# A decay built in two column parts, and four score banks for three pairs of heads, in a fused attention and two-layer MoE kernel

## Chip, cores and metric

One core of a Trainium2 chip. The metric is the device time of one execution in microseconds (us), lower is better; before the change it is 803.99 us, the median of three runs (802.63 to 804.92).

## What is computed

Attention over 32 heads (4 batches of 8), 576 tokens, head size 64, with a causal mask and a forget gate `f`; then a feed-forward layer with squared ReLU, then a second one whose hidden row goes through a softmax, a product and a layer norm:

```
scores = q @ k.T / sqrt(D)
cum    = cumsum(log(clip(f, 1e-4, 1)))
scores = where(causal, -1e9, scores + cum[:, None] - cum[None, :])
x      = softmax(scores) @ v            # 2304 x 512
g      = s * max(x @ w_in, 0)**2 + b    # first MoE, hidden size 2048
x2     = g @ w_out
h      = x2 @ w2_in                     # second MoE, hidden size 1024
out    = layer_norm(h * softmax(h)) * g_ln @ w2_out
```

## The kernel before

Heads go in 16 pairs. A pair's 576 query rows are taken in four groups: group 0 holds the query blocks 0 and 1 (256 keys at most), group 1 the last 64 rows of both heads (all 576 keys), groups 2 and 3 the blocks of 384 and 512 keys. For a group, TensorE (PE) multiplies q by k into two PSUM banks `S0` and `S1` (function `scores`, one bank a head), VectorE (DVE) adds the mask, negates and keeps each row's minimum (`unit`, L665, called a minimum below), ScalarE (ACT) takes the exponential (L710), PE transposes the result into a `PT` bank (L725), ACT or DVE copies it to `pa` or `pb` (L732, L733), and PE multiplies by v into the bank `O` (`pv`, L787).

For the first four pairs (`p < NA`, NA = 4) the decay is added on PE: a second, short product of a selector `sel` or `selt` with `dk` gives each score its key's decay. `dk` comes from one chain at the start. `f` of all 32 heads is loaded (32 x 576), clamped on DVE (L421), its logarithm taken on ACT (L423), summed along the keys by a scan on DVE (L432), and from that `decay` makes `dk384` (group 0 and 2, L428 and L429, against key 192) and `dk576` (group 1 and 3, against key 448); each is split in two rows of numbers and then copied to the other half of the partitions (L399 or L401). Later pairs take their decay from `dec` and `dect`, which are loaded from DRAM; `decay_rows` (L444) writes those rows through the `raw` tiles.

Group 0 of all four pairs goes first, then the other groups pair by pair. PSUM has, beside S, PT and O, one bank `h` and two banks of `x2` that belong to the MoE. While only group 0 of the first four pairs runs (`part`), scores go round four banks: `S0`, `S1` and the two of `x2`. All other scores use the two S banks.

The order on each engine's queue is set by a planner (`Plan.run`): every step has an engine or a choice of engines, a cost and a priority, and the planner lists the steps in the order in which its own model would start them. Every engine then runs its list strictly in order, and SyncE (SP) issues all DMAs from one list. Where PE would be idle the planner puts in products with a zero matrix (L488, called fillers). While attention runs, the weights of the MoE are loaded as 64-bit words and converted (`value`: L821 on ACT, L823, L825 and L828 on DVE), and jobs of the first MoE run between the pairs (L1064 into `h`, L1070 to L1072 into `x2`). After attention PE works on the MoEs alone.

Of the kernel before, what the change touches and what calls it, by code (L numbers as in the profile page):

```python
# [12 lines left out]
ALU = mybir.AluOpType  # L13
# [14 lines left out]
BP = 300  # L28
# [33 lines left out]
def f32(ap):  # L62
    return ap.bitcast(F32)
# [184 lines left out]
def dve2(n):  # L248
    return 69 + 0.52 * n
# [14 lines left out]
def kernel(  # L264
# [143 lines left out]
    def tt(out, a, b, n, op, r, w, pri=0):  # L408
# [2 lines left out]

    ft, one, n_ = (es[i][0:BH] for i in (1, 2, 3))
    sel_ = es[0][:, 0:BH]

    dma(ft, f.rearrange("b h s -> (b h) s"), (), [("e", 1)], BH * S * 4, -1e6)
    add("DVE", 60, lambda: nc.vector.memset(eps, 1e-9), (), ["eps"], -9e6)
    add("ACT", 1500, lambda: nc.scalar.activation(out=sm0[:, 0:1], in_=eps, func=AF.Ln), ["eps"], ["sm0"], -9e6)
    add("DVE", 200, lambda: nc.vector.memset(one, 1.0), (), [("e", 2)])  # L420
    add("DVE", 370, lambda: nc.vector.tensor_scalar(out=ft, in0=ft, scalar1=1e-4, scalar2=1.0, op0=ALU.max, op1=ALU.min),  # L421
        (), [("e", 1)], -1e5, lk=True)
    add("ACT", 573, lambda: nc.scalar.activation(out=ft, in_=ft, func=AF.Ln), (), [("e", 1)], -1e5)  # L423

    def decay(g, n0):
        t, w = dks[g], dks[g].shape[1]
        n, at = n_[:, 0:w], n_[:, n0:n0 + 1]
        nc.vector.tensor_scalar(out=t[0:BH], in0=n, scalar1=at, scalar2=None, op0=ALU.subtract)  # L428
        nc.vector.scalar_tensor_tensor(out=t[BH:2 * BH], in0=n, scalar=at, in1=f32(t)[0:BH], op0=ALU.subtract, op1=ALU.subtract)  # L429

    def decays():
        nc.vector.tensor_tensor_scan(out=n_, data0=one, data1=ft, initial=0.0, op0=ALU.mult, op1=ALU.subtract)  # L432
        decay(0, 192)

    add("DVE", 1250 + dve2(384) + dve(384), decays, [("e", 1), ("e", 2)], [("e", 3), ("dk", 0, 0)], -1e5, lk=True)
    add("DVE", dve2(S) + dve(S), lambda: decay(1, 448), [("e", 3)], [("dk", 1, 0)], 3000, lk=True)
    for g, b in enumerate((-1e5, 3000)):
        t = dks[g]
        copy(lambda t=t: t[2 * BH:4 * BH], lambda t=t: f32(t)[0:2 * BH], t.shape[1], [("dk", g, 0)], [("dk", g, 2)], b)
# [10 lines left out]
    decay_rows(0, 256, S, ((dec_d, 0, 0, 512),), "decA")  # L450
    decay_rows(1, 448, S, ((dect_d, 0, 0, S),), "decB")
# [67 lines left out]
    def split_qk(p, part, b):  # L519
# [4 lines left out]
        tt(lambda: t, lambda: r, lambda: f32(h()), n, ALU.subtract, kr + kh, kt, b)  # L524

    add("ACT", 1400, lambda: nc.scalar.activation(out=ms[0][0:BH, 0:1], in_=ft[:, 0:1], func=AF.Exp),
        [("e", 1), ("dk", 0, 2)], [("m", 0)], -9e4)

    def take(keys):

# [24 lines left out]
    def prep_dec(p):  # L555
        j = p % 2
        t, u = decs[j], dects[j]
        kd = [("decA", 0)]
        dma(t[:, :, 0:512], dec_d[p][None].broadcast_to((128, 2, 512)), kd, [("dec", j)], 524288, BP, rate=300, after=[sc_[p - 2, 1]])
        for x in range(2):  # L560
            dma(u[64 * x:64 * x + 64], dect_d[p, x][None].broadcast_to((64, S)), [("decB", 0)], [("dect", j, x)], 256 * S, BP, rate=300, after=[sc_[p - 2, 1]])
# [14 lines left out]
        add("POOL", pool2(64), lambda: nc.gpsimd.tensor_tensor(out=u[:, 512:S], in0=u[:, 512:S], in1=maskt[:, 224:288], op=ALU.add),  # L576
            ["maskt"], [("dect", j, x) for x in range(2)], BP)
# [8 lines left out]
    def scores(p, g):  # L586


        j, qbs = p % NA, [units[i][0] for i in groups[g]]
        part = g == 0 and p < NA  # L590
        one_ = p < NA
        t, h = ((lambda: whole[j]),) * 2 if one_ else ((lambda: ts[j]), (lambda: hs[j]))
        rk = [(a, j, x) for a in (("W",) if one_ else ("T", "H")) for x in ((0,) if g == 0 else PARTS)]
        if one_:
            rk += [("dk", g % 2, y) for y in (0, 2)] + [("selt", p % 2) if g == 1 else "sel"]
        (sx, kx), (sy, ky) = bank("S", part), bank("S", part)

# [24 lines left out]
        def s_mm():
            n = 2 if one_ else 3
            for i in range(n):
# [28 lines left out]
    def unit(s, p, i, two):  # L653
# [864 lines left out]
```

## Time and profile before

| | before |
|---|---|
| median of three runs | 803.99 us |
| the profiled execution | 801.1 us |
| its span, first to last instruction | 799.3 us |
| PE, DVE, ACT busy in the span | 98%, 59%, 62% |

The profiled execution took 801.1 us, of which 1.8 us lie outside the span; it is 2.9 us (0.36%) below the median of the runs shown. Times in the rows count from the span's start. The granted TensorE clock reads 0.999 over the span. A busy PE is a PE with a product under way, and that is not a PE at its peak.

### The profile page before, as it was taken

The page shows a single profiled execution, that of the slowest core. Times are in us where ns is not written, and L with a number is a line of the kernel's source. Part 1 is how long each engine was busy: PE and PEld are TensorE (multiplying, and loading weights), DVE is VectorE, ACT ScalarE, POOL GpSimd, SP SyncE. Part 2 cuts the span into 40 slices and gives each one's busy share as a digit, 9 for nine tenths or more (in the row PEclk, how much of TensorE's full clock was granted, in tenths as well). Part 3 has the DMA queues.
Part 4 walks back from the last instruction along what each step waited for, and adds up shares of the span by engine and source line. Part 5 has one row for each costly group of instructions (what it writes and reads, how often), then busy time and mean ns, then how long its engine had stood idle before and what let it go on. Part 6 is the DMA issues. An engine that isn't in the chain of part 4 may idle for free.

```text
span 799.3 us, 12785 instructions
## 1 busy us (share of the span) xinstructions
PE 779.5 (98%) x4543; PEld 642.2 (80%) x4543; DVE 474.9 (59%) x1025; ACT 495.8 (62%) x1012; POOL 126.6 (16%) x171
## 2 busy tenths in 40 slices
PE   8899999999999999999999999999999999999997
PEld 7567788778788987888878888788998788888886
DVE  8888889778783463321358765522229975665630
ACT  7788798878786676664477677645425654443441
POOL 1323222222110020100102200100002730100000
PEclk9999999999999999999999999999999999999999
DMA  8976897986943784130276875751416121000011
GB/s 273 297 230 221 264 321 243 289 300 227 286 173 121 215 284 136 36 129 1 80 236 232 273 259 185 262 238 57 128 56 235 54 66 39 22 19 27 26 40 53
DMA packets 73015, 132.59 MB, mean 166 GB/s; under 512 B 7704, under 2 KB 29848, under 8 KB 72952
## 3 DMA queue, kind: packets, MB, share of 16 engines
q1 hardware_dynamic: 72952, 131.78, 49.6%
q8 instruction: 35, 0.57, 0.3%
q14 instruction: 28, 0.23, 0.1%
HBM read 91.17 MB, written 40.58 MB: 165 GB/s over the span
## 4 chain that ended last, share of the span: by engine, by line
PE 83%; DVE 5%; issue 4%; ACT 4%; DMA 3%; POOL 1%; ACTq 0%; POOLq 0%; DVEq 0%; SPq 0%
PE h L1064 15%; PE x L1064 9%; PE ph L1273 7%; PE x2w L1072 7%; PE x2w L1070 6%; PE x2w L1071 6%; PE S L628 4%; PE po L1331 4%; PE po L1329 4%; PE po L1330 4%; PE PT L725 4%; PE O L787 4%; PE pt L1317 2%; PE x L1070 2%; PE x L1071 2%
## 5 line engine op out<-in xcount | busy, mean ns | idle before, releaser
L1012 DVE SCALAR_TENSOR_TENSOR gl<-r,b_sb,gh 128x512 fp32r<-128x512 f32 x71 | 55.2, 778 | 133.3 <-ACT gh L1021 128.1
L710 ACT ACTIVATE e<-e,m 128x128 f32<-128x128 f32 (+4 forms) x144 | 83.2, 580 | 20.8 <-DVE m L665 20.6
L1071 PE MATMUL x2w<-gl,u 128*128 128x512 f32 (+1 forms) x200 | 73.7, 368 | 0.0
L1072 PE MATMUL x2w<-gh,u 128*128 128x512 f32 (+1 forms) x200 | 73.7, 368 | 0.0
L1070 PE MATMUL x2w<-gh,u 128*128 128x512 f32 (+1 forms) x200 | 73.6, 368 | 0.0
L725 PE MATMUL PT<-ident,e 128*128 128x128 f32 x384 | 60.0, 281 | 4.1 <-ACT e L710 3.2
L1064 PE MATMUL h<-xhl,w 128*128 128x256 f32 (+1 forms) x384 | 61.0, 297 | 0.5 <-ACT r L998 0.5
L998 ACT ACTIVATE r<-h 128x512 f32<-128x512 f32 x46 | 27.3, 593 | 53.6 <-PE h L1064 53.3
L1329 PE MATMUL po<-v,dh 128*128 128x512 f32 x144 | 58.3, 405 | 0.0
L1331 PE MATMUL po<-v,dl 128*128 128x512 f32 x144 | 56.4, 392 | 0.0
L1330 PE MATMUL po<-v,dh 128*128 128x512 f32 x144 | 56.2, 390 | 0.0
L725 PEld LDWEIGHTS PT<-ident,e 128*128 128x128 f32 x384 | 42.0, 141 | 16.8 <-ACT e L710 7.4
L1321 DVE TENSOR_TENSOR dl<-pt,dh 128x512 fp32r<-128x512 f32 x36 | 24.6, 689 | 49.9 <-ACT dh L1320 49.9
L1064 PEld LDWEIGHTS h<-xhl,w 128*128 128x128 f32 x384 | 49.8, 190 | 2.9 <-ACT r L998 0.7
L1005 ACT ACTIVATE r<-r,s_sb 128x512 f32<-128x512 f32 x68 | 49.3, 724 | 2.2
L1064 PE MATMUL h<-xh,u 128*128 128x256 f32 (+1 forms) x216 | 46.1, 331 | 0.0
L1021 ACT ACTIVATE gh<-r,b_sb 128x512 fp32r<-128x512 f32 x62 | 44.7, 721 | 1.7 <-DVE r L1002 0.4
L1004 ACT ACTIVATE r<-r 128x512 f32<-128x512 f32 x68 | 43.0, 632 | 1.5
L1071 PEld LDWEIGHTS x2w<-gl,u 128*128 128x128 f32 x200 | 37.7, 189 | 6.3
L1072 PEld LDWEIGHTS x2w<-gh,u 128*128 128x128 f32 x200 | 37.7, 189 | 6.2
L1070 PEld LDWEIGHTS x2w<-gh,u 128*128 128x128 f32 x200 | 37.7, 189 | 6.2
L998 ACT ACTIVATE r<-x 128x512 f32<-128x512 f32 x26 | 15.5, 596 | 43.5 <-PE x L1064 43.5
(273 smaller groups left out, 1978.5 us busy)
## 6 DMA issues: line engine op xcount, KB each, us to landing
wraw<-in_moe_w_in_dram SPq DMA_DIRECT2D x24, 512.0 KB
wraw<-in_moe_w_out_dram SPq DMA_DIRECT2D x24, 512.0 KB
w_d<-w SPq DMA_DIRECT2D x44, 256.0 KB
raw<-in_qk_dram SPq DMA_DIRECT2D x12, 608.0 KB
dec<-dec_d SPq DMA_DIRECT2D x12, 512.0 KB
v<-w_d SPq DMA_DIRECT2D x12, 512.0 KB
vs<-in_v_dram SPq DMA_DIRECT2D x16, 320.0 KB
u_d<-wr SPq DMA_DIRECT2D x20, 256.0 KB
```

The source lines that it names most:

```text
L710: nc.scalar.activation(out=e[:, c], in_=e[:, c], func=AF.Exp, scale=-1.0, bias=m[:, j:j + 1], accum_out=rt[:, cols[j]:cols[j] + 1])
L725: nc.tensor.transpose(pt[:, kb, :], e[:, 128 * kb:128 * kb + 128], ident)
L1005: nc.scalar.activation(out=r, in_=r, func=AF.Copy, scale=s_sb)
L1012: nc.vector.scalar_tensor_tensor(out=gl, in0=r, scalar=b_sb, in1=f32(gh), op0=ALU.add, op1=ALU.subtract)
L1064: nc.tensor.matmul(t, w_, v_[:, kc, :], start=kc == 0 and first and x == 0, stop=kc == KD - 1 and x == 2, skip_group_check=True)
L1070: nc.tensor.matmul(t, a_, gh, start=start, stop=False, skip_group_check=True)
L1071: nc.tensor.matmul(t, a_, gl, start=False, stop=False, skip_group_check=True)
L1072: nc.tensor.matmul(t, b_, gh, start=False, stop=stop, skip_group_check=True)
L1273: nc.tensor.matmul(o, s_[:, kc, :], mv[:, c], start=x < 5 and kc == 0 and z == 0, stop=kc == 1 and z == 2, skip_group_check=True)
L1329: nc.tensor.matmul(ot, dh[:, j, :], wh[:, c], start=j == 0, stop=False)
L1330: nc.tensor.matmul(ot, dh[:, j, :], wl[:, c], start=False, stop=False)
L1331: nc.tensor.matmul(ot, dl[:, j, :], wh[:, c], start=False, stop=j == 7)
```

## The change

The chain of the decay is cut in two column parts, keys 0 to 255 and 256 to 575 (`HALVES`): two clamps, two logarithms, two scans, the second of which starts from column 255 of the first. `dk384` is made for its first 256 columns first, which is all that group 0 needs; then come the second scan, `dk576`, and the last 128 columns of `dk384`. The scratch tiles move from `e` (which the exponentials need) to `dect` and `dec`, which stay unused until the fifth pair's decay is loaded, and that load now waits for the chain's readers. `decay_rows` is called after group 0 and waits for the second minimum of the second pair. And scores of pairs 0 to 2 (`PW = 3`) use the four banks in all groups, not in group 0 alone; in group 0 the q-by-k products and the decay products are separate steps.

```diff
+PW = 3
-    ft, one, n_ = (es[i][0:BH] for i in (1, 2, 3))
+    ft, one, n_ = dects[1][0:BH], decs[0][0:BH, 0, 0:S], dects[0][0:BH]
-    add("DVE", 370, lambda: nc.vector.tensor_scalar(out=ft, in0=ft, scalar1=1e-4, scalar2=1.0, op0=ALU.max, op1=ALU.min),
-        (), [("e", 1)], -1e5, lk=True)
-    add("ACT", 573, lambda: nc.scalar.activation(out=ft, in_=ft, func=AF.Ln), (), [("e", 1)], -1e5)
+    HALVES = (slice(0, 256), slice(256, S))
...
+    def scan0():
+        scan(0)
+        decay(0, 192, HALVES[0], 0)
+        decay(0, 192, HALVES[0], 1)
+
+    add("DVE", 2.34 * 256 + 240 + 1.97 * 256, scan0, [("f", 0), "one"], [("n", 0), ("dk", 0, 0, 0)], -1e5, lk=True)
+    add("DVE", 2.34 * (S - 256), lambda: scan(1), [("f", 1), "one", ("n", 0)], [("n", 1)], 0, lk=True)
+    for g, n0, c, x, b in ((0, 192, HALVES[0], 0, -1e5), (1, 448, slice(0, S), 1, 1000), (0, 192, slice(256, 384), 1, 2000)):
...
-            [("e", 3)], [("raw", j, x) for x in range(3)], 3000, lk=True)
+            [("n", 0), ("n", 1)], [("raw", j, x) for x in range(3)], 3000, lk=True, after=[sm_[1, 1]])
...
+        after = [sc_[p - 2, 1]] + (list(range(*init_)) if p < NA + 2 else [])
...
-        (sx, kx), (sy, ky) = bank("S", part), bank("S", part)
+        (sx, kx), (sy, ky) = bank("S", part or p < PW), bank("S", part or p < PW)
...
+        if part:
+            add("PE", 8 * mm(256), lambda: s_mm((0,)), [("W", j, 0)], [kx, ky], sn[0] - 0.1)
+            add("PE", 2 * mm(256) + DRAIN, lambda: s_mm((1,)), rk, [kx, ky], sn[0])
+            return (sx, kx), (sy, ky)
...
     for p in range(NA):
         attention(p, (0,))
+    decay_rows(0, 256, S, ((dec_d, 0, 0, 512),), "decA")
+    decay_rows(1, 448, S, ((dect_d, 0, 0, S),), "decB")
```

The planner lays all lists out anew. The first place is DVE's list from the clamp to the first minima. `dk_129` is `dk384`, `dk_130` is `dk576`, `raw_127` and `raw_128` take the rows of `decay_rows`; before:

```order
L421 TENSOR_SCALAR e<-e 32x576
L432 SCALAR_TENSOR_TENSOR e<-e 32x576
L428 TENSOR_SCALAR dk_129<-e 32x384
L429 SCALAR_TENSOR_TENSOR dk_129<-e,dk_129 32x384
L428 TENSOR_SCALAR dk_130<-e 32x576
L429 SCALAR_TENSOR_TENSOR dk_130<-e,dk_130 32x576
L444 TENSOR_SCALAR raw_127<-e 32x576
L444 TENSOR_SCALAR raw_128<-e 32x576
L665 ISA e,m_144<-S_161,mask 128x128
```

The same place now, where `dect_160` holds `f`, `dec_157` the ones and `dect_159` the sums:

```order
L425 TENSOR_SCALAR dect_160<-dect_160 32x256
L425 TENSOR_SCALAR dect_160<-dect_160 32x320
L433 SCALAR_TENSOR_TENSOR dect_159<-dec_157,dect_160 32x256
L440 TENSOR_SCALAR dk_129<-dect_159 32x256
L442 SCALAR_TENSOR_TENSOR dk_129<-dect_159,dk_129 32x256
L433 SCALAR_TENSOR_TENSOR dect_159<-dec_157,dect_159,dect_160 32x320
L440 TENSOR_SCALAR dk_130<-dect_159 32x576
L440 TENSOR_SCALAR dk_129<-dect_159 32x128
L442 SCALAR_TENSOR_TENSOR dk_130<-dect_159,dk_130 32x576
L686 ISA e,m_144<-S_161,mask 128x128
```

`raw_127` and the last step of `dk_129` now stand behind the eight minima of the first two pairs, and `raw_128` behind those of the third pair's group 0.

The second place is PE's list at pair 0's groups 2 and 3 (`S` are the two S banks, `qk_123` is pair 0, `qk_124` pair 1); before:

```order
L628 MATMUL S_161<-qk_123 128x384
L628 MATMUL S_162<-qk_123 128x384
...
L628 MATMUL S_161<-qk_123 128x512
L628 MATMUL S_162<-qk_123 128x512
...
L628 MATMUL S_161<-qk_124 128x288
```

Now, with `x_117` the two banks of `x2`:

```order
L645 MATMUL x_117<-qk_123 128x384 x2
...
L645 MATMUL x_117<-qk_124 128x288 x2
...
L645 MATMUL S_161<-qk_123 128x512
L645 MATMUL S_162<-qk_123 128x512
...
L645 MATMUL S_161<-qk_124 128x384
```

Neighbouring groups now lie in different banks, and pair 1's group 1 stands ahead of pair 0's group 3.

## Rows read from the trace of the kernel before

**Rows 1.** The page's first part, PE alone: busy time, share of the span, instructions.

```profile
PE 779.5 (98%) x4543; PEld 642.2 (80%) x4543; DVE 474.9 (59%) x1025; ACT 495.8 (62%) x1012; POOL 126.6 (16%) x171
```

**Rows 2.** Windows: stretch, length, busy us of each engine, granted clock, DMA share, GB/s.

```profile
10.00:20.00 10.00, 8.95 (x69) 6.94 (x70) 9.13 (x45) 10.00 (x40) 0.85 (x1) 1.00 0.83 278
20.00:60.00 40.00, 35.97 (x239) 24.50 (x239) 33.64 (x80) 33.11 (x77) 11.28 (x10) 1.00 0.83 264
100.00:300.00 200.00, 196.85 (x1548) 163.39 (x1545) 142.91 (x354) 154.72 (x382) 38.47 (x48) 1.00 0.75 246
```

**Rows 3.** Timeline of DVE: start us, us, instruction, and the idle time before it.

```profile
3.35 0.45 DVE L421 TENSOR_SCALAR e<-e 32x576 f32<-32x576 f32 x1
4.55 1.35 DVE L432 TENSOR_TENSOR_SCAN e<-e 32x576 f32<-32x576 f32 x1 [0.75 <-ACT e L423]
5.93 0.41 DVE L428 TENSOR_SCALAR dk<-e 32x384 fp32r<-32x384 f32 x1
6.37 0.61 DVE L429 SCALAR_TENSOR_TENSOR dk<-e,dk 32x384 fp32r<-32x384 f32 x1
7.01 0.51 DVE L428 TENSOR_SCALAR dk<-e 32x576 fp32r<-32x576 f32 x1
7.55 0.81 DVE L429 SCALAR_TENSOR_TENSOR dk<-e,dk 32x576 fp32r<-32x576 f32 x1
8.39 1.35 DVE L444 TENSOR_SCALAR raw<-e 32x576 f32<-32x576 f32 x2
9.68 0.27 DVE L665 CUSTOM_DVE_ANT_0 e<-S,mask 128x128 f32<-128x128 f32 x1
...
12.68 0.42 DVE L733 COPY pa<-PT 128x256 f32<-128x256 f32 x1 [0.71 <-PE PT L725]
```

**Rows 4.** Timeline of ACT: the logarithm, the copy of dk, and what follows.

```profile
3.83 0.68 ACT L423 ACTIVATE e<-e 32x576 f32<-32x576 f32 x1 [0.48 <-DVE e L421]
7.01 0.51 ACT L399 CAST dk<-dk 64x384 fp32r<-64x384 f32 x1 [2.50 <-DVE dk L429]
...
9.98 0.40 ACT L710 ACTIVATE e<-e,m 128x128 f32<-128x128 f32 x1 [0.95 <-DVE m L665]
...
22.65 0.67 ACT L821 ACTIVATE wr<-wraw 128x512 f32<-128x512 f32 x1
24.29 0.62 ACT L710 ACTIVATE e<-e,m 128x384 f32<-128x384 f32 x1 [0.97 <-DVE m L665]
```

**Rows 5.** Timeline of PE: the last filler before the first scores, and pair 2's scores.

```profile
6.11 0.41 PE L488 MATMUL h<-zero 128*128 128x256 f32 x1
...
10.56 1.13 PE L628 MATMUL S<-qk 64*128 64x256 f32 x6 [1.39 <-DVE m L665]
```

**Rows 6.** Timeline of SP: the first reload of a weight buffer.

```profile
18.22 0.90 SPq L815 DMA_DIRECT2D wraw<-in_moe_w_out_dram  x1
```

**Rows 7.** Waits of ACT, then of PE, 20 to 60 us: total, times, longest.

```profile
ACT e L710 <- DVE m L665: 4.6, 4, 1.5
...
PE PT L725 <- ACT e L710: 2.3, 3, 1.4
```

**Rows 8.** Groups by line, 0 to 300 us: count, busy us, mean ns of one.

```profile
L409 DVE TENSOR_TENSOR qk<-raw,qkh 128x1216 fp32r<-128x1216 f32 x12 | 17.0, 1420 | 0.3 <-ACT qkh L399 0.3
...
L399 ACT CAST qkh<-raw 128x1216 fp32r<-128x1216 f32 x12 | 14.5, 1208 | 1.8 <-PE S L628 1.8
```

**Rows 9.** Timeline of POOL: a 512-wide copy, a subtraction, one step at two times.

```profile
50.24 0.40 POOL L573 TENSOR_SCALAR_AFFINE_SELECT dec<-dec 128x256 f32<-128x256 f32 x1
...
71.65 0.72 POOL L401 TENSOR_SCALAR w<-wr 128x512 fp32r<-128x512 f32 x1 [1.90 <-DVE wr L828]
72.46 1.29 POOL L410 TENSOR_TENSOR w<-wr,w 128x512 fp32r<-128x512 f32 x1
...
93.49 1.38 POOL L573 TENSOR_SCALAR_AFFINE_SELECT dec<-dec 128x256 f32<-128x256 f32 x1
```

**Rows 10.** Timeline of DVE: the two-input step beside the POOL step of 93.49 us.

```profile
93.29 1.32 DVE L409 TENSOR_TENSOR xhl<-xraw,xhl 128x1024 fp32r<-128x1024 f32 x1
```

More of the change, by code (lines that the diff above doesn't have):

```diff
@@ L410, in tt @@
              "POOL": (pool2(n), lambda: nc.gpsimd.tensor_tensor(out=out(), in0=a(), in1=b(), op=op))}, 0, 0, r, w, pri)
-    ft, one, n_ = (es[i][0:BH] for i in (1, 2, 3))
+    ft, one, n_ = dects[1][0:BH], decs[0][0:BH, 0, 0:S], dects[0][0:BH]
     sel_ = es[0][:, 0:BH]
-    dma(ft, f.rearrange("b h s -> (b h) s"), (), [("e", 1)], BH * S * 4, -1e6)
+    init_ = [len(P.ops)]
+    dma(ft, f.rearrange("b h s -> (b h) s"), (), ["ft"], BH * S * 4, -1e6)
     add("DVE", 60, lambda: nc.vector.memset(eps, 1e-9), (), ["eps"], -9e6)
@@ L419 @@
     add("ACT", 1500, lambda: nc.scalar.activation(out=sm0[:, 0:1], in_=eps, func=AF.Ln), ["eps"], ["sm0"], -9e6)
-    add("DVE", 200, lambda: nc.vector.memset(one, 1.0), (), [("e", 2)])
-    add("DVE", 370, lambda: nc.vector.tensor_scalar(out=ft, in0=ft, scalar1=1e-4, scalar2=1.0, op0=ALU.max, op1=ALU.min),
-        (), [("e", 1)], -1e5, lk=True)
-    add("ACT", 573, lambda: nc.scalar.activation(out=ft, in_=ft, func=AF.Ln), (), [("e", 1)], -1e5)
[L425 to L439, printed above, removed]
+    add("DVE", 200, lambda: nc.vector.memset(one, 1.0), (), ["one"])
@@ new lines @@
+    HALVES = (slice(0, 256), slice(256, S))
+    for x, c in enumerate(HALVES):
+        add("DVE", 70 + 0.66 * (c.stop - c.start), lambda c=c: nc.vector.tensor_scalar(
+            out=ft[:, c], in0=ft[:, c], scalar1=1e-4, scalar2=1.0, op0=ALU.max, op1=ALU.min), ["ft"], [("f", x)], -1e5 + x, lk=True)
+    for x, c in enumerate(HALVES):
+        add("ACT", 200 + 0.833 * (c.stop - c.start), lambda c=c: nc.scalar.activation(out=ft[:, c], in_=ft[:, c], func=AF.Ln), (), [("f", x)],
+            -1e5 + x)
@@ new lines, in scan, with decay @@
+    def scan(x):
+        c = HALVES[x]
+        nc.vector.tensor_tensor_scan(out=n_[:, c], data0=one[:, c], data1=ft[:, c], initial=n_[:, 255:256] if x else 0.0, op0=ALU.mult,
+                                     op1=ALU.subtract)
+    def decay(g, n0, c, part):
+        t = dks[g][:, c]
+        n, at = n_[:, c], n_[:, n0:n0 + 1]
+        if part == 0:
+            nc.vector.tensor_scalar(out=t[0:BH], in0=n, scalar1=at, scalar2=None, op0=ALU.subtract)
+        else:
+            nc.vector.scalar_tensor_tensor(out=t[BH:2 * BH], in0=n, scalar=at, in1=f32(t)[0:BH], op0=ALU.subtract, op1=ALU.subtract)
@@ new lines, in scan0 @@
+    def scan0():
[5 more added lines that the diff above has]
+    for g, n0, c, x, b in ((0, 192, HALVES[0], 0, -1e5), (1, 448, slice(0, S), 1, 1000), (0, 192, slice(256, 384), 1, 2000)):
+        w, t, kd = c.stop - c.start, dks[g], ("dk", g, c.start)
+        if x:
+            for part in range(2):
+                add("DVE", (90 + 0.8 * w, 150 + 1.17 * w)[part], lambda g=g, n0=n0, c=c, part=part: decay(g, n0, c, part),
+                    [("n", 0), ("n", 1)], [kd + (0,)], b, lk=True)
+        copy(lambda t=t, c=c: t[2 * BH:4 * BH, c], lambda t=t, c=c: f32(t)[0:2 * BH, c], w, [kd + (0,)], [kd + (2,)], b)
@@ L445, in decay_rows @@
             out=t, in0=n_[:, 0:w], scalar1=n_[:, n0:n0 + 1], scalar2=1.0 / scale, op0=ALU.subtract, op1=ALU.mult),
-            [("e", 3)], [("raw", j, x) for x in range(3)], 3000, lk=True)
+            [("n", 0), ("n", 1)], [("raw", j, x) for x in range(3)], 3000, lk=True, after=[sm_[1, 1]])
         for o, a, b, c in to:
             dma(o.rearrange("p x n -> (p x) n")[:, a:a + c], t[:, b:b + c], [("raw", j, x) for x in range(3)], [(keys, a)], BH * 4 * c, 3000)
-    decay_rows(0, 256, S, ((dec_d, 0, 0, 512),), "decA")
-    decay_rows(1, 448, S, ((dect_d, 0, 0, S),), "decB")
     EB = 256
@@ L526 @@
     add("ACT", 1400, lambda: nc.scalar.activation(out=ms[0][0:BH, 0:1], in_=ft[:, 0:1], func=AF.Exp),
-        [("e", 1), ("dk", 0, 2)], [("m", 0)], -9e4)
+        [("f", 0), ("f", 1), ("dk", 0, 0, 2)], [("m", 0)], -9e4)
+    init_.append(len(P.ops))
     def take(keys):
@@ L557, in prep_dec @@
         t, u = decs[j], dects[j]
+        after = [sc_[p - 2, 1]] + (list(range(*init_)) if p < NA + 2 else [])
         kd = [("decA", 0)]
-        dma(t[:, :, 0:512], dec_d[p][None].broadcast_to((128, 2, 512)), kd, [("dec", j)], 524288, BP, rate=300, after=[sc_[p - 2, 1]])
+        dma(t[:, :, 0:512], dec_d[p][None].broadcast_to((128, 2, 512)), kd, [("dec", j)], 524288, BP, rate=300, after=after)
         for x in range(2):
-            dma(u[64 * x:64 * x + 64], dect_d[p, x][None].broadcast_to((64, S)), [("decB", 0)], [("dect", j, x)], 256 * S, BP, rate=300, after=[sc_[p - 2, 1]])
+            dma(u[64 * x:64 * x + 64], dect_d[p, x][None].broadcast_to((64, S)), [("decB", 0)], [("dect", j, x)], 256 * S, BP, rate=300, after=after)
         def tri(o, w, n, base):
@@ L594, in scores @@
         if one_:
-            rk += [("dk", g % 2, y) for y in (0, 2)] + [("selt", p % 2) if g == 1 else "sel"]
-        (sx, kx), (sy, ky) = bank("S", part), bank("S", part)
+            rk += [("dk", g % 2, o, y) for o in ((0,) if g < 2 or g == 3 else (0, 256)) for y in (0, 2)] + [("selt", p % 2) if g == 1 else "sel"]
+        (sx, kx), (sy, ky) = bank("S", part or p < PW), bank("S", part or p < PW)
         def products(x, c, kc):
@@ L620, in scores, with s_mm @@
             blocks.append([(x, st[:, 0:w], w - 128, slice(0, w), True) for x, st in enumerate((sx, sy))])
-        def s_mm():
+        def s_mm(r=None):
             n = 2 if one_ else 3
-            for i in range(n):
+            for i in r or range(n):
                 for two in blocks:
@@ L666, in smin @@
                 out=e_, in0=sp, in1=mk, scale=-scale, scalar=init, op0=ALU.add, op1=ALU.min, accum_out=acc)
+        sm_[p, i] = len(P.ops)
         if p >= NA:
@@ L795, in pv @@
         return po, ko
-    state, sc_ = {}, {}
+    state, sc_, sm_ = {}, {}, {}
     def attention(p, r):
@@ L875, in stage_u @@
     def stage_u():
-        at = [sc_[p, g] for p in range(U0, NPAIR) for g in range(4)]
+        at = [sc_[p, g] for p in range(U0, NPAIR) for g in range(4) if (p, g) in sc_]
         for i, src in enumerate(x for fp in rest for x in fp_srcs(fp)):
```

## Prediction, made before the changed kernel was run

> **What bounds the kernel now.** I read the page's first part first: PE is busy 98% of the span [rows 1], so a change that leaves PE's real work alone can only win where PE stands idle or turns fillers, and the place matters. The windows show the place. From 100 to 300 us PE is busy 196.85 of 200 us, 3.15 us idle; from 20 to 60 us it is busy 35.97 of 40, 4.03 us idle, with DVE at 33.64 and ACT at 33.11; from 10 to 20 us ACT is busy 10.00 of 10 us and PE 8.95 [rows 2]. So behind about 100 us PE sets the pace, and a microsecond won ahead of it should be carried to the end nearly whole. In the first 20 us one chain sets it: clamp, logarithm, scan, `dk`, and then first minima on DVE and exponentials on ACT. The timeline of DVE shows that chain without a gap from 4.55 to the first minimum at 9.68 [rows 3]; ACT's first exponential starts at 9.98 and waited 0.95 us for it [rows 4]. PE meanwhile turns fillers until 6.11 and waits 1.39 us for pair 2 [rows 5]; what it does before that is filling.
>
> **The start, part by part.** From start to start, DVE's steps take 0.44 and 0.64 us at 384 columns and 0.54 and 0.84 us at 576 (5.93, 6.37, 7.01, 7.55, 8.39 in [rows 3]). Both pairs give a fixed 0.24 us, plus 0.52 ns a column for the first kind and 1.04 ns for the second. I give the clamp, the scan and the logarithm the same fixed part, for want of two widths of each.
>
> - Clamp of 256 columns: 0.24 + 256/576 x (0.45 - 0.24) = 0.33, so 3.35 to 3.68. Logarithm: 0.24 + 256/576 x (0.68 - 0.24) = 0.44, from 3.71 (0.03 behind the clamp, as 3.80 to 3.83 before) to 4.15. The scan starts at 4.19 instead of 4.55. The other halves of clamp and logarithm lie beside these and cost nothing: DVE is free until the scan, and the second logarithm ends at about 4.65, before the second scan wants it.
> - DVE from the scan to the first minimum, before: 9.68 - 4.55 = 5.13. Now: scan 256 0.75, `dk384` 0.37 and 0.51, scan 320 0.87, `dk576` 0.54 and 0.84, the first step of the last 128 columns 0.31, together 4.19. The two `raw` steps, 1.29 us from 8.39 to 9.68, are out of the way, and three steps more have come in, 3 x 0.24 = 0.72.
> - First minimum at 4.19 + 4.19 = 8.38: 1.30 us early. PE can serve it: the copy of the first 256 columns starts near 5.8, and the decay products follow on q-by-k products already made.
> - ACT now makes the copy of `dk576`, which POOL made before: 0.24 + 1.5 x (0.51 - 0.24) = 0.65, from about 8.38 to 9.03. Then the exponentials: 9.03 instead of 9.98, 0.95 early.
> - Behind the minima of pair 1 the last step of `dk384` (0.37) and one `raw` (0.645) come in, 1.02 us; 0.71 us of idle time stood there [rows 3], so pair 2's minima are 1.30 + 0.71 - 1.02 = 0.99 early, no less than ACT. The DMAs of those `raw` rows go out later, behind `xs_d` and `rs_d` on SP's list; their readers are the loads for the fifth pair, far behind, so I cost that at nothing.
> - Past the weights: DVE's list has the first conversion behind the fourth pair's minima now. Adding up from 8.38, L828 ends some 1.3 us later than the 18.2 at which SP reloads that buffer [rows 6]. The load was there by 22.65 [rows 4]; if it needed all of the 4.4 us, ACT waits up to 0.7 us, beside PE's work. I leave this at the low end.
>
> From 9.98 to 22.65 ACT works nearly without a gap, so what arrives is ACT's lead. ACT has one copy of `pa` more in that stretch, 512 wide, at most twice the 0.42 of [rows 3]. Lead carried on: between 0.1 (0.95 - 0.84) and 1.3; I take **0.9**, close to ACT's 0.95, because DVE is relieved by that same copy.
>
> One page speaks against cutting steps up. The 0.24 us of [rows 3] are paid by each of the three added steps. The Trainium skill (VectorE: DVE Perf Modes, the section on the TRN2 errata) says that a VectorE instruction with SBUF operands pays a fixed extra latency, 58 cycles at 0.96 GHz by its table, and advises few, long instructions. By that figure (an estimate, 60 ns each) the three would cost 0.18 instead of 0.72 and the lead on DVE would be 1.8; the trace's rows decide here, and they are steps that wait for each other.
>
> **The banks.** From 20 to 60 us ACT waits four times, 4.6 us in all, for a minimum, and PE 2.3 us for exponentials [rows 7]; the first of them is at 24.29, 0.97 us, behind pair 0's group 1 [rows 4]. With two banks the scores of the next group can't be written before this group's minima are read, so PE, DVE and ACT take turns. With four, the next group is ready when DVE is. Lower end 0: at 84% and 83% DVE and ACT have other work, and lists are strict. Upper end all of PE's 4.03 us of idle time [rows 2]. I take half, **2.0**, because only three of the pairs have the four banks, and waits for loads stay. Fillers before the first scores fall from 24 to 11; they took PE's idle time only, so no term.
>
> **The sum.** 0.9 + 2.0 = 2.9 us. Against the profiled execution, 801.1 - 2.9 = 798.2. That execution lies 2.9 below the median of the runs shown; on the median, 803.99 - 2.9 = **801.1**.
>
> **Rivals.**
>
> 1. *The lead is lost again* (803.1 to 804.9). The weights and the activations of the first MoE job come by DMA, at a share of 0.83 from 20 to 60 us [rows 2], in SP's order; if PE's list reaches the MoE products early and then waits for the same loads at the same times, start and banks give nothing net. For it: the reload that goes out 1.3 us later. Against: pairs 0 to 3 need no load after the first 17 us. Time: 803.99 less 0 to 0.9, plus up to the 0.9 by which the runs spread upwards.
> 2. *The banks give all* (799.1). PE's idle time from 20 to 60 us vanishes: 803.99 - 0.9 - 4.0. For it: the waits of [rows 7] are most of it. Against: ACT and DVE are nearly full.
> 3. *Slower: POOL gets work that PE waits for* (806.6). The new lists give POOL three of the 1216-wide copies of q and k that ACT made in 1.21 us each, and one of the subtractions that DVE made in 1.42 us [rows 8]. POOL's 512-wide copy takes 0.72 and its subtraction 1.29 [rows 9]; by width 1.71 and 3.06, so 0.50 and 1.64 more. And one POOL step of the same size took 0.40 alone and 1.38 [rows 9] beside a two-input DVE step [rows 10]: 0.98 more each. All four in full: 3 x 1.48 + 2.62 = 7.1 us. It needs PE to reach that pair's scores before POOL is done; it decides once more than the 0.9 of lead arrives at PE. With half of it, 3.5, and no gain from banks: 803.99 - 0.9 + 3.5 = 806.6. For it: the lists are strict. Against: PE has MoE products to do in between. The Trainium skill (SBUF — State Buffer, the section on who interferes with whom) says that POOL and a DVE step with two SBUF inputs exclude each other for a whole instruction; by that rule the 1.38 is a lock, and the trace agrees as far as that one pair of rows goes.
>
> **Chances.** Forecast (799.6 to 803.1) 0.48, rival 1 0.23, rival 2 0.16, rival 3 0.13. A measurement can tell about 0.3%, 2.4 us, from no change: faster is below 801.6, slower above 806.4. Some two thirds of the forecast's case lie below 801.6, 0.31, and with rival 2 faster gets 0.47. No difference: the forecast's rest and rival 1, 0.40, less 0.01 for a place I did not see: 0.39. Slower: rival 3 and that 0.01, 0.14. The range goes from 797.0 (1.3 for the start, 4.03 for the banks, half of the 3.15 idle from 100 to 300 us off 803.99) to 806.0, which takes in rival 1 and the lighter part of rival 3.
>
> **What would show it.** Right: the first minimum at 8.4 and the first exponential at 9.0; ACT's wait for minima from 20 to 60 us well below 4.6; PE's idle time there about 2 instead of 4; from 100 us on a PE as busy as before. Wrong in the start: a minimum after 9, as when the q-by-k products wait for their load. Wrong in the banks: PE's idle time in that stretch as before, now for loads, or at the POOL copies of q and k. Wrong in the whole: PE idle time moved behind 60 us.

## The result, and the profile of the changed kernel

The change makes the kernel faster: 796.20 us at the median against 803.37, six executions of each, a ratio of 0.9914 with a 95% interval from 0.9890 to 0.9938. That is 7.2 us where 2.9 were forecast; the sign was right, the size not, and the time lies 0.8 us below the range. The profiled execution took 796.63 us, with a span of 794.6 us, so the two profiles show 4.5 us of the 7.2; the other 2.7 is that the profiled execution of before, at 801.1, lies 2.3 us under its median and that of the change 0.4 over.

The page's first part for the changed kernel, against [rows 1]:

```profile
PE 777.6 (98%) x4529; PEld 639.0 (80%) x4529; DVE 475.8 (60%) x1025; ACT 491.3 (62%) x1006; POOL 137.3 (17%) x180
```

PE is busy 1.9 us less, DVE the same, and POOL 10.7 us more. The windows, against [rows 2], with two stretches more:

```profile
10.00:20.00 10.00, 10.00 (x72) 6.28 (x70) 9.04 (x36) 8.98 (x37) 0.82 (x2) 1.00 0.82 287
20.00:60.00 40.00, 38.32 (x271) 26.83 (x271) 36.45 (x86) 35.82 (x87) 16.20 (x18) 1.00 0.96 298
60.00:100.00 40.00, 38.00 (x306) 29.96 (x302) 29.82 (x82) 31.25 (x82) 18.77 (x17) 0.96 0.71 229
85.00:90.00 5.00, 4.19 (x23) 2.39 (x23) 2.79 (x5) 4.90 (x15) 5.00 (x4) 0.76 0.81 265
...
100.00:300.00 200.00, 196.41 (x1526) 163.12 (x1521) 147.81 (x354) 152.42 (x371) 39.94 (x49) 1.00 0.77 245
```

From 20 to 60 us PE does 271 products where it did 239, idle for 1.68 us instead of 4.03. From 100 us on it is as busy as before (196.41 against 196.85). So in these two profiles the time comes from the first 60 us, and from 60 to 100 us PE still stands idle for 2.00 us. The timeline of DVE shows the start, against [rows 3]:

```profile
3.35 0.52 DVE L425 TENSOR_SCALAR dect<-dect 32x256 f32<-32x256 f32 x2
4.12 0.68 DVE L433 TENSOR_TENSOR_SCAN dect<-dec,dect 32x256 f32<-32x256 f32 x1 [0.25 <-ACT dect L428]
4.83 0.34 DVE L440 TENSOR_SCALAR dk<-dect 32x256 fp32r<-32x256 f32 x1
5.21 0.47 DVE L442 SCALAR_TENSOR_TENSOR dk<-dect,dk 32x256 fp32r<-32x256 f32 x1
5.71 0.87 DVE L433 TENSOR_TENSOR_SCAN dect<-dec,dect,dect 32x320 f32<-32x320 f32 x1
6.62 0.70 DVE L440 TENSOR_SCALAR dk<-dect 32x576 fp32r<-32x576 f32 x2
7.35 0.81 DVE L442 SCALAR_TENSOR_TENSOR dk<-dect,dk 32x576 fp32r<-32x576 f32 x1
8.19 0.29 DVE L686 CUSTOM_DVE_ANT_0 e<-S,mask 128x128 f32<-128x128 f32 x1
...
10.53 0.34 DVE L442 SCALAR_TENSOR_TENSOR dk<-dect,dk 32x128 fp32r<-32x128 f32 x1
10.91 0.51 DVE L462 TENSOR_SCALAR raw<-dect 32x576 f32<-32x576 f32 x1
```

The first minimum stands at 8.19, 1.49 us earlier. ACT's timeline, against [rows 4], has the long copy of `dk` and then the first exponential at 8.89, 1.09 us earlier:

```profile
8.19 0.67 ACT L400 CAST dk<-dk 64x576 fp32r<-64x576 f32 x1 [0.56 <-DVE dk L442]
8.89 0.40 ACT L732 ACTIVATE e<-e,m 128x128 f32<-128x128 f32 x1
```

In the waits from 20 to 60 us, ACT's wait for minima, 4.6 us in [rows 7], is nearly gone, and a load stands ahead of it:

```profile
ACT wr L843 <- DMA wraw<-in_moe_w_in_dram: 1.6, 1, 1.6
...
PE PT L747 <- ACT pb L754: 0.5, 1, 0.5
...
ACT e L732 <- DVE m L686: 0.3, 1, 0.3
```

**What PE's idle time does not show.** The groups by line have the fillers (L488 before, L503 now). Before, 0 to 60 us:

```profile
L488 PE MATMUL x<-zero 128*128 128x256 f32 x23 | 6.9, 393 | 1.0 <-DVE eps L418 1.0
L488 PE MATMUL h<-zero 128*128 128x256 f32 x9 | 3.6, 401 | 0.0
```

With the change, the same view and stretch:

```profile
L503 PE MATMUL h<-zero 128*128 128x256 f32 x12 | 2.8, 330 | 0.0
L503 PE MATMUL x<-zero 128*128 128x256 f32 x8 | 2.7, 436 | 1.0 <-DVE eps L420 1.0
```

A filler counts as busy, and it stands where PE has nothing else to do. In the first 60 us they fell from 10.5 to 5.5 us, and PE's idle time from 6.95 to 3.93 (60 less 53.05 and 56.07 busy). That is at most 8.0 us more for work; a filler's record overlaps with its neighbours', so the sum is an upper value.

So I counted PE's work itself: of every group by line and shape in a stretch, its count times the time from start to start of such a product in a dense stretch (about 0.1 us for a PT product, 0.12 for h from `xhl`, 0.19 for a 288-wide score, and so on), fillers at nothing. The **lead** at a time is by how much earlier a kernel has done what the kernel before has done by then. At 60 us before has 42.3 us of work behind it; the change has 38.4 at 50 us and 47.6 at 60, so it reached 42.3 at 54.3: a lead of 5.7. The change's lead is 2.1 at 20 us, 5.7 at 60, 4.7 at 100, and 4.7 at the end (799.3 less 794.6). Up to 80 us it repeats: a second profile of the same kernel gave 2.1, 5.4 and 5.9 at 20, 60 and 80 us where the first gave 2.1, 5.7 and 5.5. Behind that it does not (1.7 against 3.8 at 275 us), so one profile's lead there says little. Other weights drawn from the same traces move a lead at 60 us by about 1 us: read it to the microsecond, not to the tenth.

### The profile page after: what moved, and what is told of

It reads as the page before. It is cut to its first block, busy times and chain, and to the rows that moved or that the text cites. A ratio compares the mean times of both kernels' runs of the same rounds, so it can differ in the third digit from the quotient of the medians.

```text
span 794.6 us, 12767 instructions
## 1 busy us (share of the span) xinstructions
PE 777.6 (98%) x4529; PEld 639.0 (80%) x4529; DVE 475.8 (60%) x1025; ACT 491.3 (62%) x1006; POOL 137.3 (17%) x180
## 4 chain that ended last, share of the span: by engine, by line
PE 81%; DVE 7%; DMA 5%; ACT 3%; issue 2%; SPq 1%; POOL 0%; DVEq 0%; ACTq 0%; POOLq 0%
PE h L1086 15%; PE x L1086 9%; PE ph L1295 7%; PE x2w L1093 7%; PE x2w L1094 7%; PE x2w L1092 7%; PE po L1353 4%; PE po L1351 4%; PE po L1352 4%; PE S L645 4%; PE O L809 3%; PE PT L747 3%; DMA xo<-rs_d 2%; PE pt L1339 2%; PE x L1092 1%
## 5 line engine op out<-in xcount | busy, mean ns | idle before, releaser
L686 DVE CUSTOM_DVE_ANT_0 e<-S,dec 128x128 f32<-128x128 f32 (+2 forms) x72 | 34.3, 508 | 20.6 <-PE S L645 20.4
L1092 PEld LDWEIGHTS x2w<-gh,u 128*128 128x128 f32 x200 | 37.7, 189 | 6.3
```

Source lines behind the costliest of these rows:

```text
L1092: nc.tensor.matmul(t, a_, gh, start=start, stop=False, skip_group_check=True)
```

## The experiments

The expectations of the first four runs set theories A, B and C against each other, which put the missing microseconds in different places: A leaves the start at the 0.9 us of the prediction and looks in the banks, the others look elsewhere, what new lists do by themselves among it (any edit draws up the lists anew). D was formed after these four: start and banks give the lead of the first 60 us together, and the lists decide how much of it is lost at the loads that come behind. All runs, with the lead at 20, 60 and 100 us from each run's profile:

| run | ratio to before | 95% interval | lead at 20, 60, 100 us |
|---|---|---|---|
| the change | 0.9914 | 0.9890 to 0.9938 | 2.1, 5.7, 4.7 |
| the change, again | 0.9917 | 0.9885 to 0.9950 | 2.1, 5.4, 3.8 |
| change, DRAIN 250 | 0.9890 | 0.9857 to 0.9923 | 2.1, 6.2, 4.6 |
| change, DRAIN 230 | 0.9905 | 0.9875 to 0.9936 | 2.1, 6.2, 4.0 |
| before, DRAIN 250 | 0.9981 | 0.9962 to 1.0001 | 0.0, 0.3, 0.0 |
| before, DRAIN 230 | 1.0008 | 0.9979 to 1.0037 | 0.0, 0.1, -5.6 |
| decay alone | 1.0003 | 0.9984 to 1.0022 | 1.7, 2.3, -1.6 |
| decay alone, DRAIN 250 | 1.0003 | 0.9983 to 1.0023 | 1.7, -0.2, -4.2 |
| banks alone | 0.9964 | 0.9945 to 0.9982 | -0.6, 2.4, 3.2 |
| banks alone, DRAIN 250 | 0.9917 | 0.9879 to 0.9955 | 1.1, 3.3, 3.2 |
| decay, banks for 1 pair | 0.9988 | 0.9962 to 1.0014 | 2.1, 0.1, 0.1 |
| decay, banks for 2 pairs | 0.9947 | 0.9919 to 0.9976 | 1.9, 3.3, 1.5 |
| decay, banks for 4 pairs | 0.9859 | 0.9810 to 0.9908 | 2.1, 5.3, 6.6 |
| 4 pairs, DRAIN 250 | 0.9837 | 0.9810 to 0.9865 | 2.1, 6.0, 7.7 |
| 4 pairs, DRAIN 230 | 0.9826 | 0.9793 to 0.9859 | 2.1, 6.3, 8.2 |
| decay, banks for 5 pairs | 0.9825 | 0.9796 to 0.9854 | 2.1, 5.4, 7.7 |
| change, nothing wide on POOL | 1.0018 | 0.9999 to 1.0037 | 2.1, 5.0, -0.2 |

**One part at a time.** The decay alone is the change with the banks taken back:

```
-PW = 3
+PW = 0
```

> The changed kernel with PW = 0: the decay in two parts stays, all scores outside group 0 of the first four pairs go back to two banks. Theory A (the start gives about 1 us, the banks give the rest, and the two add up): 1 us under the kernel before, 802 to 803 where that one takes 803.4; first exponential at 8.9 us; ACT's wait for minima from 20 to 60 us back near 4.6 us. Theory B (the new start gives most, because the scratch tiles no longer hold the exponentials' tiles): 797 to 798.5. Theory C (what counts is that the planner lays out all lists anew, and any edit can do that): no relation, 797 to 806.

802.48 us at the median, 1.0003 of the kernel before on the same chip: the start alone is worth nothing at the end, although its lead stands at 2.3 us at 60 us. The first exponential is at 8.90, as expected. ACT's wait for minima from 20 to 60 us is not: with two banks again it should have been back near 4.6 us, and it is 1.3:

```profile
ACT e L732 <- DVE m L686: 1.3, 1, 1.3
```

So that wait does not tell whether a kernel has the banks. PE's idle time in that stretch does so far: 3.45 us here, against 4.03 before and 1.68 with the change. The windows show that and where the lead went:

```profile
20.00:60.00 40.00, 36.55 (x251) 26.31 (x249) 36.05 (x82) 33.45 (x76) 13.70 (x13) 1.00 0.87 266
0.00:60.00 60.00, 53.81 (x363) 38.88 (x365) 53.39 (x147) 49.77 (x128) 16.78 (x30) 1.00 0.85 270
60.00:100.00 40.00, 35.59 (x278) 27.01 (x275) 32.71 (x79) 30.25 (x75) 15.03 (x15) 1.00 0.76 241
```

From 60 to 100 us PE is idle for 4.41 us. The waits there have PE waiting for exponentials, ACT for minima, and POOL for a load:

```profile
ACT e L732 <- DVE m L686: 3.5, 5, 1.4
PE PT L747 <- ACT e L732: 2.6, 4, 1.5
...
POOL xraw L411 <- DMA xo<-rs_d: 2.5, 1, 2.5
```

The banks alone are the kernel before with the banks of the change:

```
-        (sx, kx), (sy, ky) = bank("S", part), bank("S", part)
+        (sx, kx), (sy, ky) = bank("S", part or p < 3), bank("S", part or p < 3)
```

> The kernel before with one edit: scores of pairs 0 to 2 go round four banks in all groups. Theory A: about 6 us under the kernel before, 797 to 798.5; first exponential at 10.0 as before; ACT's wait for minima from 20 to 60 us under 1 us; pair 1's group 1 scores several us earlier than 27.8. Theory B: 802 to 803.4. Theory C: anything from 797 to 806, and the waits for minima do not tell the time.

799.86 us, 0.36% less than before, where 797 to 798.5 was expected. ACT's wait for minima from 20 to 60 us is 1.7 us, expected under 1. So the banks are the larger part, but less than the 7 us by themselves in this list. The scores of pair 1's group 1 were to come several us ahead of 27.8, and they start at 27.23. PE's timeline has them in the kernel before, with the decay alone, with the banks alone and in the change, in this order:

```profile
27.78 1.36 PE L628 MATMUL S<-qk 128*128 128x288 f32 x4 [0.18 <-DVE m L665]
```

```profile
29.20 1.14 PE L645 MATMUL S<-qk 128*128 128x288 f32 x4
```

```profile
27.23 1.14 PE L628 MATMUL x<-qk 128*128 128x288 f32 x4
```

```profile
21.63 1.24 PE L645 MATMUL x<-qk 128*128 128x288 f32 x4 [0.17 <-DVE m L686]
```

The starts of these 288-wide scores for each of the first four pairs, in us, with some of the runs that follow:

| run | pair 0 | pair 1 | pair 2 | pair 3 |
|---|---|---|---|---|
| before | 15.92 | 27.78 | 42.91 | 56.00 |
| decay alone | 15.31 | 29.20 | 41.81 | 55.72 |
| banks alone | 17.53 | 27.23 | 38.17 | 50.19 |
| decay, banks for 1 pair | 15.31 | 28.11 | 42.06 | 54.38 |
| decay, banks for 2 pairs | 15.37 | 21.70 | 32.79 | 48.60 |
| the change | 15.30 | 21.63 | 32.17 | 47.64 |

Pair 1 comes 6 us earlier only where both parts of the change are there and the first two pairs have the four banks. Either part alone leaves it here within 1.5 us of where it was. In the other lists that follow, pair 1 stands at 28.00 and 27.84 before, 29.02 with the decay alone, 25.61 with the banks alone and twice at 21.64 with the change. So for the lists tried this does not hang on the list. It fits that the gains of the two parts alone, none and 0.36%, do not add up to the 0.86% of the change.

**Lists drawn up anew.** DRAIN is one of the planner's costs; a value 10 ns off changes no work and gives other lists.

```
-DRAIN = 240
+DRAIN = 250
```

> The kernel before with the planner's cost of a drain set from 240 to 250 ns: no operation is added or removed, but lists may come out in another order. Theories A and B: within 1.5 us of the kernel before. Theory C: 3 us or more away from it in either direction.

0.9981, 2.2 us below the kernel before and so between the two expectations, with an interval that reaches 1.0001; the lead is 0.3 us at 60 us and, in the one profiled execution, 3.8 at 275. A further run took one of the lists' choices away: no subtraction or addition of 1024 columns or more goes to POOL any more, which is where the profile of the change shows rival 3 in a small form. At 81.41 us POOL takes 2.72 us for a 1024-wide step of `xraw` that waited for its load; ACT waits for it, and PE for ACT. POOL, then ACT, then PE in their timelines:

```profile
81.41 2.72 POOL L411 TENSOR_TENSOR xraw<-xraw,xo 128x1024 f32<-128x1024 f32 x1 [3.22 <-DMA xo<-rs_d]
```

```profile
84.16 1.05 ACT L400 CAST xhl<-xraw 128x1024 fp32r<-128x1024 f32 x1 [0.94 <-POOL xraw L411]
```

```profile
85.76 0.93 PE L747 MATMUL PT<-ident,e 128*128 128x128 f32 x4 [1.23 <-ACT e L732]
```

```
+        if n >= 1024:
+            del ways["POOL"]
```

> The changed kernel, but products and subtractions of 1024 columns and more may not go to POOL. In the changed kernel's trace one such step (2.72 us on POOL where DVE takes 1.23) stands at 81.4 us ahead of a copy on ACT, the exponentials behind it come late, PE idles 1.2 us and its granted clock falls to 0.76 and 0.90 from 85 to 95 us. If that place costs what it seems to: 1.5 to 3 us under the changed kernel, 793 to 795, and no fall of the granted clock there. If the planner's other moves eat it: 796 as the changed kernel, within 1 us.

803.66 us: the gain is gone, and both expectations failed. The lead is still 5.0 at 60 us and -1.0 at 90, and the granted clock falls again, to 0.66 from 85 to 90 us. The waits of this run from 60 to 100 us:

```profile
PE S L648 <- DVE m L689: 3.1, 4, 1.7
...
ACT wr L846 <- DMA wraw<-in_moe_w_out_dram: 2.5, 1, 2.5
```

So this run does not tell what the wide POOL steps cost the change: taking them off POOL gave another list, and in that list ACT waits 2.5 us for a weight load and PE 3.1 us for minima. An edit that leaves the lead at 60 us as it was can lose all of it by 90 us.

So none of the first three theories stands whole: A's size for the banks alone was missed (2.9 us measured in that list), B fell, and of C the part behind 60 us is left. That is how D came about, and the next four runs put both kernels and the banks into other lists (the edit is the line on DRAIN above).

> The changed kernel with the planner's cost of a drain at 250 instead of 240 ns, a neutral edit. Lead: by how much PE has done the same work, fillers left out, earlier than in the profile of the kernel before; the changed kernel has 2.1 us at 20 us, 5.7 at 60 and 3.8 at 275. Theory D (the early lead belongs to the change; what is kept of it behind 60 us, where loads are waited for, hangs on the list): lead at 20 us 2.1, at 60 us 4.5 to 6.5, time 794 to 802. Theory C (the lists as a whole are luck): lead at 60 us anywhere from 0 to 6.

> The changed kernel with that cost at 230 ns. As for the run with 250: theory D lead at 20 us 2.1, at 60 us 4.5 to 6.5, time 794 to 802; theory C lead at 60 us anywhere from 0 to 6.

> The kernel before with that cost at 230 ns. Theory D: lead at 20 and 60 us within 1 us of zero (the edit with 250 had 0.0 and 0.3), time 798 to 806. Theory C: lead at 60 us anywhere from -3 to 5.

> The kernel before with four banks for pairs 0 to 2 and that cost at 250 ns. Theory D: lead at 20 us about zero, at 60 us 1.5 to 3.5 as in the run with the banks alone (2.4), time 796 to 803. Theory C: lead at 60 us anywhere from -3 to 5.

The change kept 0.9890 and 0.9905, a lead of 2.1 at 20 us and 6.2 at 60 in both. The kernel before got 1.0008, no lead at 60, and lost 5.6 us by 100 in its profiled execution (PE idle for 6.08 us from 60 to 100 us), though that did not show in its median. The banks alone went from 0.9964 to 0.9917, the largest move that the DRAIN edit made; their intervals just overlap, and with two lists the banks' own worth is only known as 3 to 7 us. What the split decay adds beside the banks is no better known: 0.50% in the lists of DRAIN 240 (0.9964 to 0.9914, intervals apart), 0.27% in those of DRAIN 250 (0.9917 to 0.9890, intervals that overlap).

**By the pair.** The number of pairs with four banks is one constant. One pair:

```
-PW = 3
+PW = 1
```

> The changed kernel with four banks for the first pair alone. Theory D (start 2.1 us at 20 us, banks the rest of the lead at 60 us): lead over before in PE's work 2 at 20 us and 3 to 4 at 60 us; ACT waits for minima from 20 to 60 us between 0.3 and 1.3 us; time 797 to 801. Theory A (the start gives no more than 0.9, pairs count alike): lead at 60 us 0.9 + a third of the banks' share, under 2.2.

Two pairs, `PW = 2`:

> The changed kernel with four banks for the first two pairs. Theory D: lead at 60 us between that with one pair and the 5.7 us with three, about 4.5 to 5.2; time 796 to 799. If all of the lead comes with the first two pairs, whose scores stand before the MoE products fill PE, it is 5.7 already and the third pair counts for nothing.

Four pairs, `PW = 4`:

> The changed kernel with four banks for the first four pairs. Theory D: PE's remaining idle time from 20 to 60 us (1.68 us) is not at minima any more (ACT waits for them 0.3 us), so the lead at 60 us stays at 5.2 to 6.2 and the time within 1.5 us of the change's. If banks go on paying by the pair, lead 6.9 or more and 794 to 795.

And none, in the list of DRAIN 250:

> The split decay alone (two banks for all pairs), with the lists drawn up again by a constant that is neutral for the program (DRAIN 250 for 240). Theory D: lead 2.1 us at 20 us and 2 to 2.5 at 60 us as in the first plan without the banks; what is left at 100 us depends on the list, so 797 to 804. If the loss at 70 to 100 us (to -2.4 us at 90 us) belongs to the split decay itself, it is there again, and the time is 801 to 804.

The medians are 800.67, 798.66 and 791.57 us, and 802.55 for none. With none, one, two, three and four pairs the ratios are 1.0003, 0.9988, 0.9947, 0.9914 and 0.9859: about 0.36% or 2.9 us a pair on average, without an end at three. The intervals of neighbours overlap, so the single steps are not known. Four expectations failed. With one pair the lead at 60 us is 0.1 us, not 3 to 4, and with two it is 3.3, not 4.5 to 5.2. With four it is 5.3 at 60 us as expected, but the time is 4.6 us below the change's, not 1.5 at most: something is gained behind 60 us. The run without banks lost even the start's lead, which was to be 2 to 2.5 us at 60, by 40 us: -1.3 us there. Its windows show why that cost so much:

```profile
30.00:36.00 6.00, 4.15 (x21) 2.05 (x21) 3.77 (x9) 5.12 (x11) 1.30 (x1) 0.83 1.06 303
36.00:42.00 6.00, 6.00 (x41) 4.17 (x37) 4.85 (x11) 4.08 (x10) 1.30 (x1) 0.89 0.77 260
```

PE is idle for 1.85 us from 30 to 36 us, and the granted clock of these two stretches is 0.83 and 0.89. These are means of two levels; the same view for parts of them:

```profile
34.00:37.00 3.00, 3.00 (x14) 1.58 (x13) 1.49 (x5) 1.53 (x3) 0.00 (x0) 0.50 1.07 402
38.00:42.00 4.00, 4.00 (x29) 2.63 (x27) 3.11 (x8) 3.72 (x9) 1.30 (x1) 1.00 0.68 203
```

From 34 to 37 us PE works without a gap at 0.50, the lower level (1.2 GHz). The groups by line of 30 to 42 us have the 320-wide products of `pb` at 693 ns:

```profile
L809 PE MATMUL O<-pb,vs 128*64 128x320 f32 x12 | 4.1, 693 | 0.6 <-ACT pb L754 0.6
```

In the change, at a granted clock of 1.00, they take 441 (10 to 60 us):

```profile
L809 PE MATMUL O<-pb,vs 128*64 128x320 f32 x36 | 6.0, 441 | 0.4 <-ACT pb L754 0.4
```

**Was four pairs a lucky list?** The last four runs put it into two more lists, with the change beside it on the same chip, and gave a fifth pair the banks.

> The changed kernel itself, beside the next three on one chip, as their yardstick. Every theory: 0.989 to 0.994 of the time before.

`PW = 4` with `DRAIN = 250`, and with `DRAIN = 230`:

> Four pairs with four banks, DRAIN 250. If banks pay by the pair (about 3 us each), 0.984 to 0.989 of the time before, and PE's lead at 100 us 1.5 us or more above the change's 4.7. If the run with DRAIN 240 was a lucky list, 0.989 to 0.994 as with three pairs.

> Four pairs with four banks, DRAIN 230. As for the run before: 0.984 to 0.989 if banks pay by the pair, 0.989 to 0.994 if that list was luck.

`PW = 5`:

> Five pairs with four banks. If banks pay by the pair without end, 787 to 789 us. If they pay only while PE has to wait for minima ahead of the stretch where it sets the pace (it is 96% busy or more behind the fourth pair), 790 to 794 as with four pairs.

No luck: 0.9837 and 0.9826, a little better than the 0.984 to 0.989 expected, with intervals that end at 0.9865 where that of the change on the same chip begins at 0.9885. Four pairs beat both kernels, with medians of 791.51 and 790.41 us against 798.49 for the change. The fifth adds nothing (790.58 us). The windows of four pairs with DRAIN 230:

```profile
60.00:100.00 40.00, 38.91 (x321) 31.61 (x318) 35.68 (x81) 32.41 (x83) 14.06 (x15) 1.00 0.80 245
100.00:300.00 200.00, 199.01 (x1529) 165.61 (x1528) 142.50 (x346) 155.28 (x373) 32.33 (x45) 1.00 0.79 247
```

PE is idle for 1.09 us from 60 to 100 us and for 0.99 from 100 to 300. Four or five pairs are busy for 38.91 to 39.27 us of the first of these stretches in all four profiles; three pairs for 36.81 to 38.00 in four profiles, no more than the kernel before with its 37.92. What is earlier with four pairs is the attention. The last 512-wide scores of the fourth pair, in PE's timeline, first in the kernel before, then in the change, then with four pairs (DRAIN 250):

```profile
63.16 1.13 PE L628 MATMUL S<-qk 64*128 64x512 f32 x4
```

```profile
55.82 1.13 PE L645 MATMUL S<-qk 64*128 64x512 f32 x4
```

```profile
49.76 1.13 PE L645 MATMUL x<-qk 64*128 64x512 f32 x4
```

They move by 7.3 and then by 6.1 us more, while PE's lead at 60 us hardly differs between the last two (5.7 and 6.0): the same amount of work is done, but more of it is attention and less MoE products. Which MoE products are kept back, and that these are what fills the gaps behind 60 us, is read from this and was not tried by itself.

Over all eighteen profiles, PE's idle time from 20 to 60 us goes with the banks: 2.87 to 4.03 us in the five with two banks, 3.60 with four banks for one pair, and 1.24 to 2.54 in the twelve with four banks for more. ACT's wait for minima there does not: 4.0 to 5.0 us in the three of the kernel before, 0.4 and 1.3 with the decay alone, and from none to 1.8 with the change and with four or five pairs.

## Why the prediction was wrong in size

- **The start.** Right in its steps: first minimum 8.38 predicted and 8.19 measured, first exponential 9.03 and 8.89, scan at 4.19 and 4.12. The added 128-wide step takes 0.38 us from start to start (10.53 to 10.91), where 0.24 plus 1.04 ns a column gives 0.37. The rule from the Trainium skill (VectorE: DVE Perf Modes, the section on the TRN2 errata), with its 58 cycles, would have given 0.06 plus the same slope, 0.19; the row decides against it for steps that wait for each other. What was carried was not "0.9" but 1.7 to 2.1 us of PE's work at 20 us. By then PE had turned 17 fillers instead of 27: it did the q-by-k products where fillers had stood. "They took PE's idle time only, so no term" left that out. Yet by itself it came to nothing in both lists (1.0003 twice): lost at 60 to 100 us in the one and at 20 to 40 in the other. The step "a microsecond won ahead of it should be carried to the end nearly whole" failed between 60 and 100 us, a stretch that the argument went past.
- **The banks.** This is the step that failed: "Upper end all of PE's 4.03 us of idle time" and "I take half, **2.0**". The term was 2.0; between the decay alone and the change the runs show 0.9% at the end, some 7 us, and 1.1% in the lists of DRAIN 250. The idle time itself went much as forecast, from 3.45 to 1.68 us between these two from 20 to 60 us. But it was the wrong measure of what the banks are worth, in two parts. In the first 60 us the lead grows by 3.4 us, of which 2.26 us is idle time (6.19 to 3.93) and up to 1.2 us fillers (6.7 to 5.5); that is still below the 4.03 us of the cap. It goes beyond the cap behind 60 us, where the sum has no term at all: at 100 us the two are 6.3 us apart in lead, because the decay alone has lost 3.9 us of its lead since 60 us and the change 1.0. What differs there is the attention: the last scores of the third and the fourth pair come 11.3 and 7.3 us earlier than before (52.17 to 40.91 and 63.16 to 55.82; with the decay alone the first of these still stands at 51.03). That PE then has more in hand where others make it wait is how I read this second part; the runs by the pair bear it out, without showing it by itself. And one of the signs was not the banks' own: ACT's wait for minima is 1.3 us with the decay alone and 0.3 with the change, so most of its fall from 4.6 came without them. That the sum took start and banks apart was a third fault: pair 1's scores come 6 us earlier only with both.
- **A page that bears on it.** PE was busy 98% and that measure led the argument [rows 1]. The Trainium skill (Perfetto Trace Analysis, Identifying the Most-Contended Engine) calls TensorE's matmul busy time a poor measure of how close a kernel is to its limit, and would look at MFU, the arithmetic done against the peak, and at the weight loads. The trace agrees with the first half: the busy time held 10.5 us of fillers in the first 60 us. Of the two others the weight loads would not have helped here: PEld rose only from 38.95 to 39.76 us in that stretch while 5.3 us more work was done, and fillers load weights too. Counting the work, as the lead does, is nearer to the first.
- **Rival 1** (the lead is lost to loads, 803.1 to 804.9) is what happens to the decay alone, 802.48 and 802.55 us, and to the change without wide work on POOL, 803.66. The loss came true there, and not for the change as a whole. That loads cause it is not shown: PE's waits of the decay alone from 60 to 100 us name exponentials (2.6 us) and minima (1.6 us), and ACT waits 2.8 us there for weight loads, which no run took away.
- **Rival 2** (the banks give all, 799.1) named the larger part and had the same false cap.
- **Rival 3** (POOL gets wide work that PE waits for, 806.6) did not come about with the four steps it names: no engine is seen to wait for one of them. Another wide step, at 81.41 us, stood ahead of 1.23 us of PE's idle time. The copies were overpriced: POOL's 1216-wide copies took 1.22 us, not 1.71 by width; the subtraction took 2.80, near the 3.06. The collision that it prices on POOL seems to have cost DVE at one of them: beside the first copy a two-input DVE step takes 1.68 us, where the five others of its line from 19.55 to 53.23 us take 0.68 or 0.69. POOL, then DVE in their timelines:

```profile
33.18 1.22 POOL L402 TENSOR_SCALAR qkh<-raw 128x1216 fp32r<-128x1216 f32 x1 [0.80 <-DMA raw<-in_qk_dram]
```

```profile
33.26 1.68 DVE L850 SCALAR_TENSOR_TENSOR wr<-wraw,wr 128x512 uint32<-128x512 uint32 x1
```

- **The chances.** "Faster" at 0.47 was the largest and came true; the range ended at 797.0 because more than half of its lower end hung on the idle time from 20 to 60 us (4.03 of 1.3 + 4.03 + 1.6 us).

Open: why the stretch behind 60 us costs one list 5 us of lead and another 1, and whether a single transfer does it. One profile overstates it, too: before with DRAIN 230 and with DRAIN 250 are 9.5 us apart in their profiled spans (803.8 and 794.3) and 0.27%, 2.2 us, in their ratios.

## What to carry to other kernels

An engine that turns fillers or stands behind drawn-out products is "busy", so idle time is no upper bound for what a change can give it: count the products, not the busy share. A second pair of buffers between two engines can pay for longer than the idle time shows: here through the fourth pair, and not for the fifth. Try one step more than the change made, and stop where the next adds nothing. When a scheduler draws up new lists for every edit, run each version in two or three lists before a difference of half a per cent is believed.

## What the runs showed of the hardware that I had not expected

Idle time of PE can be followed by slower products, some microseconds later. With the decay alone in the list of DRAIN 250, PE stood idle for 1.19 and 1.23 us, until 28.52 and 31.65 us; the granted clock was still 1.00 to 33 us and then 0.50 from 34 to 37, with PE busy all the time, and the 320-wide products took 693 ns instead of 441. In the change the 1.23 us of idle time end at 85.76 us, and the granted clock is 0.50 from 88 to 91:

```profile
88.00:91.00 3.00, 3.00 (x15) 1.66 (x15) 0.63 (x4) 2.55 (x7) 2.56 (x2) 0.50 0.39 124
```

It is not always so: before the change PE waits 1.39 us until 10.56 [rows 5], and the granted clock stays at 1.00 from 10 to 20 us [rows 2].

POOL's copy, where nothing holds it up, costs about 0.83 ns a column and 0.2 us besides: over all runs the shortest copies take about 0.62 us at 512 columns, 1.04 at 1024 and 1.20 at 1216. Many take longer: of 398 copies at 512 columns 162 stay below 0.70 us, and the 0.72 us of [rows 9] does not. One of the short ones, in the change:

```profile
61.67 0.62 POOL L402 TENSOR_SCALAR w<-wr 128x512 fp32r<-128x512 f32 x1 [2.78 <-DVE wr L850]
```

At 1216 columns it is as fast as ACT's copy of 1.21 us [rows 8].
